# A late permutation in four wide matmuls, useless matmuls in TensorE's waits, and a residual moved behind the second MLP layer

## The chip, the cores and the metric

The kernel runs on one core of one Trainium2 chip. The metric is the device time of one execution in microseconds (us), given as the median of several executions.

Names in the profile: PE is TensorE's matmuls, PEld its weight loads, DVE is VectorE, ACT is ScalarE, SP the engine that issues transfers. The tiles: ring holds keys, values and weights as they land, PS is PSUM, O_sb is the copy of a unit's value result out of PSUM, SEL stands for the matmuls that pick that copy's rows by head, oTn the normalised result, KTb a work buffer, W2 the weights of the second MLP layer. A "fill" is a useless matmul.

## The reference, cut to what matters

One decoding step of a transformer block for 8 sequences: modulation, layer norm, attention of one new token over a cache of 8192 keys and values (8 key-value heads, 32 query heads, 128 wide), output projection and residual, then a second layer norm, a squared-ReLU MLP (512 to 1792 to 512) and the last residual.

```python
o = softmax(q @ k_cache.T / sqrt(128)) @ v_cache       # per batch and head; 268 MB of keys and values
x = x + ga * (o.reshape(B, 1, Hq * Dh) @ wo)
h = layernorm(x) * (1 + cb) + sb
x = x + gb * (relu(h @ w1 + b1) ** 2 @ w2 + b2)
```

## The kernel before

Keys and values stream through a ring of four 4 MB slots. For each batch there are four key units (transpose on TensorE, copy out, score), the softmax, and four value units. In the last batch the last value unit comes in chunks and is followed by the tail: projection of the last two heads, second layer norm, MLP, output. The parts that the change and the argument touch, with cuts marked:

```python
def pe_stream(n, at):      # n useless bf16 matmuls of 512 columns into bank `at`
def pe_stream32(n, at):    # the same in fp32: one each 0.94 us ahead of unit 2 in the trace before, against 0.22
...
# softmax of each batch
pe_stream32(1, 4)                                   # fills a wait for VectorE
T_ps = bank(7)[:, 0:4]
...
# value units p = 0..3 of a batch
def values(a, z, stop):                             # one matmul: 4 key tiles, 32 weight columns, 512 moving
    for m in range(a, z):
        cg = m % 4                                  # four column groups run beside each other
        t = op("tensor", lambda e, ...: e.matmul(Obank[32 * cg:32 * (cg + 1), :], lhs[...], vt[...],
               tile_position=(0, 32 * cg)), ...)
...
if p == NP - 3: pe_stream32(1, 4)                   # after unit 1's values
elif p == NP - 2: pe_stream(2, 4)                   # after unit 2's values
...                                                 # copy O_sb, four SEL matmuls
if p == NP - 3: pe_stream32(2, 4)                   # after unit 1's SEL, ahead of unit 2
...
# last value unit: CH = (64, 112, 120, 128)
t = values(16, 28, 24)                              # 12 matmuls
t = op("vector", ... tensor_copy(osb, bank(3)))     # copy O_sb
direct(CH[1], CH[2], 2)                             # one matmul per key tile, beside the copy
...                                                 # SEL, direct(CH[2], CH[3], 3), oTn
k_oP = permute(3, 4, oP[:, 0:2], [t])               # 16 matmuls of 16 columns, one copy of 128x64
...                                                 # 32 late projection matmuls, norm, first layer
for f in range(FT):                                 # second layer, 14 blocks of 4 matmuls
    if f == 8:
        ...                                         # residual: 4 matmuls of x1T with the identity
    for k in range(KT):
        t = op("tensor", ... matmul(yT_ps[:, k, :], W2v[:, f, ...], hidT[:, f, :]), [..., d_w2[f // 4]])
k_y2 = op("vector", ...)                            # y2, then 4 matmuls add it to the residual
```

## Time and profile before

| what | before |
|---|---|
| time, median of 3 (range) | 668.69 us (668.61 to 668.72) |
| span of the traced run | 666.6 us |
| first key transpose of the last batch | 585.91 us |
| clock back at full after it | 590.08 us |
| value unit 2 lands; its first matmul | 644.13; 644.18 us |
| last piece of W2 lands | 662.98 us |

The transfers fill the span; only the end of the last batch is compute that nothing hides. Two things help in reading the rest. First, everything behind value unit 2 is a single chain, so I give its events as distances from unit 2's first matmul. Second, TensorE's clock is full (1.00) or half (0.50), one value per window of 3.413 us. These are the windows in which the last batch's keys begin, before the change (after the stretch: busy time of PE, PEld, DVE, ACT and POOL with instruction counts, then granted clock, DMA share, GB/s):

```profile
583.25:586.67 3.42, 0.76 (x8) 0.77 (x9) 0.00 (x0) 0.00 (x0) 0.00 (x0) 0.50 1.07 460
586.67:590.08 3.41, 3.41 (x35) 3.41 (x34) 1.92 (x3) 1.02 (x1) 0.00 (x0) 0.50 0.96 413
590.08:593.49 3.41, 3.41 (x60) 2.88 (x59) 2.13 (x4) 2.33 (x3) 0.00 (x0) 1.00 0.98 423
```

And these are the early projection and the first value matmuls of the last unit behind it, at full clock, which c3 will be compared with:

```profile
649.11 1.48 PE PS L550 x24
650.59 0.86 PE PS L641 x16
```

In the windows above, the core waited for keys, fell to half clock, and got the full clock back 4.17 us after its first transpose: 35 matmuls in a window at half clock, 60 in the next.

### The profile page before, as it was taken

The page shows a single profiled execution, that of the slowest core. Times are in us where ns is not written, and L with a number is a line of the kernel's source. Part 1 is how long each engine was busy: PE and PEld are TensorE (multiplying, and loading weights), DVE is VectorE, ACT ScalarE, POOL GpSimd, SP SyncE. Part 2 cuts the span into 40 slices and gives each one's busy share as a digit, 9 for nine tenths or more (in the row PEclk, how much of TensorE's full clock was granted, in tenths as well). Part 3 has the DMA queues.
Part 4 walks back from the last instruction along what each step waited for, and adds up shares of the span by engine and source line. Part 5 has one row for each costly group of instructions (what it writes and reads, how often), then busy time and mean ns, then how long its engine had stood idle before and what let it go on. Part 6 is the DMA issues. An engine that isn't in the chain of part 4 may idle for free.

```text
span 666.6 us, 15803 instructions
## 1 busy us (share of the span) xinstructions
PE 518.3 (78%) x7201; PEld 350.3 (53%) x7201; DVE 308.0 (46%) x586; ACT 264.0 (40%) x305; POOL 20.4 (3%) x79
## 2 busy tenths in 40 slices
PE   3309987899769976699748987399776997589876
PEld 2207753677338742477317753287434773177534
DVE  1105662367326751367314663166523673156622
ACT  2104661265316651266314661156512663146620
POOL 7400000000000000000000000000000000000000
PEclk9999999799979999799987999799987999879996
DMA  9999999999999999999999999999999999999997
GB/s 377 435 412 437 419 429 432 429 433 435 433 427 433 438 427 433 431 433 431 431 436 427 433 433 436 429 429 435 433 431 431 436 429 431 433 436 427 431 425 283
DMA packets 12188, 283.85 MB, mean 426 GB/s; under 512 B 1260, under 2 KB 1296, under 8 KB 3600
## 3 DMA queue, kind: packets, MB, share of 16 engines
q1 hardware_dynamic: 12128, 283.65, 99.3%
q8 instruction: 9, 0.15, 0.1%
q10 hardware_dynamic: 48, 0.02, 0.0%
q14 instruction: 3, 0.02, 0.0%
HBM read 283.66 MB, written 0.01 MB: 426 GB/s over the span
## 4 chain that ended last, share of the span: by engine, by line
PE 55%; DMA 32%; ACT 6%; DVE 4%; issue 1%; POOL 0%; ACTq 0%; SPq 0%; DVEq 0%; POOLq 0%
PE PS L488 38%; DMA ring<-in_A_k_cache_dram 21%; PE PS L505 10%; DMA wo_sb<-in_A_wo_dram 7%; ACT P_sb L587 5%; DMA ring<-in_A_v_cache_dram 4%; PE PS L641 3%; ACT KTb L493 1%; DVE O_sb L659 1%; DVE m L512 1%; PE PS L599 1%; PE PS L550 1%; PE PS L619 0%; DVE Pm L613 0%; PE PS L478 0%
## 5 line engine op out<-in xcount | busy, mean ns | idle before, releaser
L488 PE MATMUL PS<-IDENT,ring 128*128 128x128 bf16 x4096 | 267.8, 228 | 60.7 <-DMA ring<-in_A_k_cache_dram 33.3
L488 PEld LDWEIGHTS PS<-IDENT,ring 128*128 128x128 bf16 x4096 | 247.3, 102 | 108.9 <-issue 49.4
L493 ACT ACTIVATE KTb<-PS 128x1024 bf16<-128x1024 bf16 x192 | 196.7, 1024 | 236.1 <-PE PS L488 236.1
L495 DVE COPY KTb<-PS 128x1024 bf16<-128x1024 bf16 x320 | 210.2, 688 | 151.6 <-PE PS L488 149.4
L505 PE MATMUL PS<-KTb,Qb 128*32 128x512 bf16 x1024 | 78.8, 384 | 4.5 <-ACT KTb L493 4.5
L641 PE MATMUL PS<-ring,Pm 128*32 128x512 bf16 x1020 | 66.9, 407 | 17.9 <-DMA ring<-in_A_v_cache_dram 15.2
L659 DVE CAST O_sb<-PS 128x512 bf16<-128x512 f32 x31 | 21.4, 692 | 106.9 <-PE PS L641 106.9
L641 PEld LDWEIGHTS PS<-ring,Pm 128*32 128x32 bf16 x1020 | 27.2, 102 | 53.5 <-DMA ring<-in_A_v_cache_dram 23.0
L542 ACT ACTIVATE KTb<-PS 32x192 bf16<-32x192 f32 x16 | 5.2, 322 | 103.6 <-PE PS L472 103.4
L587 ACT ACTIVATE P_sb<-PS,negm 128x1024 bf16<-128x1024 f32 x32 | 35.2, 1112 | 20.2 <-DVE negm L583 20.2
L478 PE MATMUL PS<-ONES 128*128 128x512 f32 x80 | 42.1, 630 | 0.0
L599 PE MATMUL PS<-IDENT,P_sb 128*128 128x128 bf16 x256 | 19.8, 220 | 17.2 <-ACT P_sb L587 17.2
L613 DVE COPY Pm<-PS 64x512 bf16<-64x512 bf16 x48 | 20.2, 421 | 25.0 <-PE PS L599 24.5
L599 PEld LDWEIGHTS PS<-IDENT,P_sb 128*128 128x128 bf16 x256 | 14.4, 98 | 27.9 <-ACT P_sb L587 27.9
L505 PEld LDWEIGHTS PS<-KTb,Qb 128*32 128x32 bf16 x1024 | 15.4, 94 | 21.0 <-ACT KTb L493 8.5
L512 DVE TENSOR_REDUCE m<-PS 128x1 f32<-128x512 f32 x32 | 22.1, 689 | 6.6 <-PE PS L505 6.6
L663 PEld LDWEIGHTS PS<-SEL,O_sb 128*128 128x128 bf16 x124 | 5.8, 97 | 31.3 <-DVE O_sb L659 31.3
L550 PE MATMUL PS<-wo_sb,KTb 128*32 128x512 bf16 x192 | 15.4, 467 | 6.8 <-ACT KTb L542 6.8
L663 PE MATMUL PS<-SEL,O_sb 128*128 128x8 bf16 x124 | 7.8, 169 | 14.1 <-DVE O_sb L659 14.1
L478 PEld LDWEIGHTS PS<-ONES 128*128 128x128 f32 x80 | 12.7, 190 | 10.6 <-issue 10.6
L472 PE MATMUL PS<-IDENT 128*128 128x512 bf16 x48 | 15.7, 381 | 0.0
L550 PEld LDWEIGHTS PS<-wo_sb,KTb 128*32 128x32 bf16 x192 | 5.9, 108 | 14.0 <-DVE KTb L544 9.5
(137 smaller groups left out, 147.1 us busy)
## 6 DMA issues: line engine op xcount, KB each, us to landing
ring<-in_A_k_cache_dram SPq DMA_DIRECT2D x32, 4096.0 KB, 31.4
ring<-in_A_v_cache_dram SPq DMA_DIRECT2D x31, 4096.0 KB, 27.4
ring<-in_A_wq_dram SPq DMA_DIRECT2D x1, 4096.0 KB, 20.1
wo_sb<-in_A_wo_dram SPq DMA_DIRECT2D x1, 4096.0 KB, 46.8
ring<-in_w_mod_dram SPq DMA_DIRECT2D x1, 3072.0 KB, 10.7
ring<-in_A_v_cache_dram SPq DMA_DIRECT2D x1, 2048.0 KB, 22.9
ring<-in_A_v_cache_dram SPq DMA_DIRECT2D x1, 1536.0 KB, 26.3
ring<-in_B_w_dram SPq DMA_DIRECT2D x3, 512.0 KB, 19.1
```

The lines of the kernel that those rows point to most:

```text
L478: ts = [op("tensor", lambda e: e.matmul(bank(at).rearrange("p (a r) -> p a r", a=4), ONES[:, :], rhs)) for _ in range(n)]
L488: t = op("tensor", lambda e, j=j, i=i: e.matmul(STG[j][:, i, :], src[:, 32 * k + 8 * j + i, :], IDENT[:, :], is_transpose=True), [loaded[n ...
L493: stg_free[j] = op("scalar", lambda e, j=j, dst=dst: e.activation(dst, STG[j], ACT.Copy), [t])
L495: stg_free[j] = op("vector", lambda e, j=j, dst=dst: e.tensor_copy(dst, STG[j]), [t])
L505: t = op("tensor", lambda e, hf=hf, q=q, rhs=rhs: e.matmul(PS[32 * q:32 * (q + 1), k, :], Qb[:, 2 * p + hf, :], rhs, start=(p == 0 and hf ...
L512: return op("vector", lambda e: e.tensor_reduce(m4[:, k:k + 1], bank(k), AX.X, ALU.max), [t])
L550: t = op("tensor", lambda e, g=g, j=j: e.matmul(bank(7)[32 * j:32 * (j + 1), :], oPe[:, 3 * (g % 2) + g // 2, :, :].rearrange("p j b -> p ...
L587: exps.append(op("scalar", lambda e, k=k: e.activation(P_sb[:, k, :, :, :], bank(k).rearrange("p (i x) -> p i x", i=8).unsqueeze(2).to_bro ...
L599: t = op("tensor", lambda e, k=k, i=i: e.matmul(STG[k][:, i, :], P_sb[:, k, i, :, :].rearrange("p h x -> p (h x)"), IDENT[:, :], is_transp ...
L613: done.append(op("vector", lambda e, dst=dst, frm=frm: e.tensor_copy(dst, frm), [t, k_pm]))
L641: t = op("tensor", lambda e, m=m, cg=cg, p=p, vt=vt, Obank=Obank: e.matmul(Obank[32 * cg:32 * (cg + 1), :], lhs[:, p, 32 * m:32 * m + 32], ...
L659: t = op("vector", lambda e, osb=osb, Obank=Obank: e.tensor_copy(osb, Obank), [t])
```

## The change

Its intent: fewer and wider matmuls in the last permutation, with its copy split over two engines; TensorE kept busy in the softmax and around value unit 2 so that its clock stays up; a chunk boundary moved; and the residual matmuls taken out of the middle of the second layer. The diff, cut to its core:

```diff
-        CH = (64, 112, 120, 128)
+        CH = (64, 104, 120, 128)
...
-        def permute(q0, q1, dst, deps):           # 16 matmuls into 4 column groups, one copy
-        def permute_early(deps):                  # 4 matmuls of 192 columns, one fill, 4 copies
+        def permute(pP, q0, q1, dst, deps, fill): # for both: 4 matmuls of 64*n columns, `fill` fills,
+                                                  # 2 copies on VectorE and 2 on ScalarE, 32 partitions each
...
             pe_stream32(1, 4)
+            pe_stream(1, 4)                       # twice in the softmax
...
-            turn_acts(pe_stream(2, 1))
+            turn_acts(pe_stream(3, 1))
...
-            pe_stream(1, 1)
+            pe_stream(2, 1)
...
-                    proj_done = project(permute_early([norm_last, k_all] + stg_free + hold))
+                    proj_done = project(permute(..., 0, 3, oPe, [norm_last, k_all] + stg_free + hold, 3))
...
                     elif p == NP - 2:
-                        pe_stream(2, 4)
+                        pe_stream(3, 4)
...
+                    elif p == NP - 2:             # after unit 2's SEL
+                        pe_stream(1, 4)
...
-                    t = values(16, 28, 24)
+                    t = values(16, CH[1] // 4, 22)
...
-                    k_oP = permute(3, 4, oP[:, 0:2], [t])
+                    k_oP = permute(bank(6)[:, 0:256]..., 3, 4, oP, [t], 0)
...
         for f in range(FT):
-            if f == 8:
-                ...                               # the four residual matmuls
             for k in range(KT):
                 ...
+        for cc in range(2):
+            ...                                   # the four residual matmuls
```

## The prediction

> **What bounds the kernel now.** I read the page's busy row and its DMA part first, then the chain that ended last in order of time, then the clock by windows.
>
> ```profile
> PE 518.3 (78%) x7201; PEld 350.3 (53%) x7201; DVE 308.0 (46%) x586; ACT 264.0 (40%) x305; POOL 20.4 (3%) x79
> ...
> q1 hardware_dynamic: 12128, 283.65, 99.3%
> ...
> HBM read 283.66 MB, written 0.01 MB: 426 GB/s over the span
> ```
>
> The DMA queue fills 99.3% of the span; no compute engine comes near. So the bulk of the 666.6 us is the time to read 283.66 MB, and the change reads the same bytes. Compute can matter only where it finishes after the data, so I followed the chain from the place where it last hangs on a transfer:
>
> ```profile
> 616.37 27.77 DMA ring<-in_A_v_cache_dram
> 644.13 0.04 issue
> 644.18 1.94 PE PS L641 x32
> ...
> 652.88 0.79 PE PS L641 x12
> ...
> 653.70 0.70 DVE O_sb L716
> ...
> 654.45 0.25 PE PS L719 x4
> 654.70 0.23 PE PS L693 x8
> ...
> 654.95 0.20 DVE oTn L723
> ...
> 655.20 0.39 PE PS L523 x14
> ...
> 655.61 0.24 DVE KTb L527
> ...
> 662.61 0.31 PE PS L774 x4
> 662.92 0.75 PE PS L778 x24
> ```
>
> Columns are start, length, what. The last value unit but one lands at 644.13; from there the chain is TensorE and VectorE work to the end, 22 us in which no step waits long for data. That is the only stretch where this change can move the time, so all it can win or lose is tenths of a microsecond of 668.69. The transfers are close behind the chain, though. The trace's semaphore records put the last chunk of values at 654.09 and the last piece of W2 at 662.98, and its last eight matmuls start near 663.3. In windows (after the stretch: each engine's busy time, then granted clock, DMA share, GB/s):
>
> ```profile
> 651.52:654.93 3.41, 2.89 (x51) 2.10 (x50) 0.69 (x1) 0.00 (x0) 0.00 (x0) 1.00 1.01 392
> 654.93:658.34 3.41, 1.75 (x56) 1.49 (x57) 1.35 (x8) 0.00 (x0) 0.00 (x0) 0.50 1.03 405
> ...
> 662.00:663.00 1.00, 1.00 (x32) 0.77 (x30) 0.14 (x1) 0.00 (x0) 0.00 (x0) 0.50 0.26 90
> 663.00:664.00 1.00, 0.72 (x26) 0.63 (x26) 0.19 (x1) 0.00 (x0) 0.00 (x0) 0.50 0.00 0
> ```
>
> The clock falls to 0.50 at 654.93 and stays there for the whole tail, and the DMA is in use until 663.
>
> **What the Trainium skill says.** (1) "TensorE: Matmul & The Clock Gate", Part 1: the clock is halved or full according to activity in a free-running window of 3413 ns. The trace agrees: all its changes lie at whole multiples of 3.413 us from each other (576.43, 579.84, 583.25, 590.08, 654.93). I added up, per window, the streamed columns at 2.4 GHz, weighted by the columns of the array in use: every window before a fall has at most 0.36 and every window that keeps the full clock 0.38 or more. The window 651.52 to 654.93 has 0.27; the two before it have 0.64. (2) Same page, same part: starts of small matmuls are never closer than about 25 ns. The trace agrees: eight-column matmuls follow each other every 25.0 ns at full clock and 26.7 ns at half, so half clock costs such matmuls only 7%; the 16-column ones take 33 ns instead. (3) "ScalarE: Activation LUTs", What ACT_TABLE_LOAD costs: 0.833 ns per element plus a fixed part. Here 192 elements took 322 ns (L542) and 256 took 375 (L793), 0.83 per element. The one table load in the tail took 1283 ns, as the page has it. (4) "PSUM — Partial Sum Buffer", Terms: two engines must not be in one bank and quadrant at once, different quadrants are allowed. The early copies (L542, L544) already run beside each other on such quadrants at 648.3, so the four late ones may too.
>
> **The change part by part.**
>
> *Useless matmuls.* A 128x512 bf16 matmul streams for 0.213 us (512 at 2.4 GHz). Softmax of each batch gets four more, unit 2 two more, the early permutation two more. Each sits in an idle piece of TensorE: after unit 2's values the copy O_sb takes 0.69 us (646.14 to 646.83), and three streams (0.64 us, begun at 646.02) end streaming by 646.66; behind the early permutation three end by 648.52, while its copies run to 648.97; in the softmax the gaps are 0.20, 0.72, 0.42 and 0.33 us against 0.21. Path: 0 (at worst 0.05). What they could buy is clock, but the windows they fill (up to 648.9) have 0.64 already, far over the 0.37 that decides, and the window that brings the fall begins at 651.52 and gets none. Gain: 0.
>
> *Chunks 64/104/120/128.* Two fewer of the 512-column value matmuls (12 to 10). Four run at once, 0.053 us each on average: 0.11 us less before the copy O_sb. Eight more direct matmuls (27 ns each) lie beside that copy's 0.69 us. The second chunk is 262 KB smaller and lands about 0.6 us earlier than 652.76, so no new wait. The weight of activity in the decisive window hardly changes (2 x 512 x 1/4 columns against 8 x 32: the same 256), so the clock still falls near 655. Path: -0.11.
>
> *Late permutation.* Before: 16 matmuls, 0.39 us, and one copy of 224 ns. After: 4 matmuls of 64 columns at half clock, 53 ns of streaming each and a record of about 0.21 us for the last: about 0.40 + 0.05. Then two copies in a row on each of two engines. VectorE: 64 elements took 224 ns (L527), twice with a 31 ns gap as at L544, 0.48 us. ScalarE: 375 less 192 x 0.83 gives 216 ns, twice plus some 0.04 of wait and gap, about the same. So copies 0.48 against 0.22, and permute +0.07. Path: +0.33. It is a loss. ScalarE's table load for the square root now comes behind these copies (about 656.2 to 657.5); it is needed at 660.19, so hidden.
>
> *Residual behind the second layer.* In the before-trace the last matmul of block 7 starts at 662.444 and the first of block 8 at 662.856: 0.41 us for four residual matmuls where a 26.7 ns step would do. Removing them wins 0.385 us in that place. The four now run in the 0.28 us between the last layer-2 matmul and y2, streaming about 0.21 us (two at a time, 107 ns at half clock): hidden. But with blocks 8 to 13 moved up, the last piece of W2 (landing 662.98, start possible at about 663.03) would be needed at 662.90: the transfer takes over. From 663.03 eight matmuls end at 663.41 instead of 663.66: at most -0.25 without help from upstream or from a faster DMA.
>
> *Sum.* Upstream: -0.11 + 0.33 = +0.22. Block 12 starts at 662.90 + 0.22 = 663.12, just behind its data; the end moves by 663.12 - 663.28 = -0.16 us. If the late permutation costs less, the W2 transfer holds the gain at -0.25, less some 0.04 that one larger piece instead of a 2 KB-per-row one may save (the two 262 KB chunks landed 0.65 to 0.68 us apart, 385 to 403 GB/s, against 410 to 423 for the pieces behind them). Centre: -0.2 us, so 668.5.
>
> **Rivals.** (a) *The clock stays up in the tail.* For it: the fall comes from a window that is only 0.10 short, and its phase is free-running, so in another run the fall could come up to 3.4 us later. Against: fills end before that window. If it happened, some 58 sixteen-column and other matmuls at 25 instead of 27 to 33 ns, and fixed parts, would save perhaps 0.5 us of TensorE time upstream, but W2's landing at 662.98 would cap the total at about -0.3: 668.4. The four runs before lie within 0.11 us, so phase cannot be worth much. (b) *The new copies on ScalarE wait longer* (a late wake-up, or the table load placed before them: 1.28 us). It would put the time at 668.8, or 669.5 with the load; the compiler places the load ahead of the instruction that needs it, so I give that 4%. (c) *Fills delay work*: unit 2's start at 644.18 follows fills that end at 644.08, so 0.1 us of delay in the softmax would show, but no more than 0.1: 668.6. (d) *Everything hidden by the transfer*: the last W2 landing decides and the time is 668.4.
>
> **Range and chances.** The four cases lie between 668.4 and 668.8; add 0.1 us of scatter as before and some for another chip: 668.2 to 668.85. Two per cent would be 13 us; nothing on the path is so large, so within 2% is 0.99.
>
> **What would show it.** In the changed trace, measured from unit 2's landing: the copy O_sb of the last unit 0.1 us sooner; from oTn to the first matmul of the late projection about 1.0 us instead of 0.75; the granted clock still 0.50 from a window's edge near 655; no gap between blocks 7 and 8 of layer 2, but a wait for the W2 transfer (or almost one) before block 12; y2 some 0.2 us sooner after W2's landing. I am wrong if the full clock lasts into the tail, if the late permutation is not slower, or if unit 2 itself starts late.

## More of the kernel before

The change and its causes are tenths of a microsecond in 668, so besides medians I use times within a trace, counted from one event of it.

L641 is line 641 of the kernel; lines shift by up to ten between versions, so I name the work as well.

## The result, and the profile after

| | before | changed |
|---|---|---|
| median of 4 runs | 668.71 us | 668.53 us |
| range | 668.61 to 668.81 | 668.20 to 669.24 |
| unit 2's first matmul (traced run) | 644.18 us | 645.25 us |
| from there to the end of the span | 22.47 us | 22.26 us |
| granted clock falls in the tail | 654.93 us | 656.84 us |

The ratio is 0.9999, with a 95% interval of 0.9981 to 1.0016. Ratios here are the mean time of one kernel's runs over that of the other's of the same rounds, so they are not quite the ratio of the medians.

Two things stand beside each other. The tail became 0.21 us shorter. But the traced run of the changed kernel is its slowest, 669.24 us, and there unit 2 began 1.07 us later than in the trace before: its data landed 0.65 us later (644.79 against 644.13), and it started 0.41 us after landing plus 0.05. The chain of the changed kernel in order of time (start, length, what) shows both:

```profile
643.42 0.08 PE PS L658 x4
643.50 1.82 PE PS L478 x4
645.32 1.87 PE PS L634 x32
...
653.96 0.77 PE PS L634 x10
...
654.75 0.70 DVE O_sb L713
...
656.01 0.20 DVE oTn L720
...
656.25 0.30 PE PS L522 x4
...
656.58 0.21 DVE KTb L535
...
656.83 0.23 DVE KTb L535
657.06 0.12 issue
657.18 1.01 PE PS L727 x32
...
662.86 1.66 PE PS L769 x56
664.52 0.31 PE PS L774 x4
664.83 0.41 PE PS L782 x4
```

Read it against the chain shown in the prediction. Before, a transfer stood ahead of unit 2; here it is L478, the useless fp32 matmuls, that unit 2 follows. (A piece of the chain begins where the record before it ends, here 645.32; the first matmul itself started at 645.25.) Ten value matmuls (L634) take 0.77 us where twelve took 0.79. The late permutation (L522) takes 0.30 us, then two copies of 0.21 and 0.23 in a row, so the late projection starts 1.17 us after oTn did, against 0.94 before. The second layer (L769) is one piece of 1.66 us, and the residual (L774) comes behind it.

The windows of the changed kernel at the start of the last keys, and in its tail:

```profile
585.16:588.57 3.41, 2.03 (x20) 2.03 (x21) 0.69 (x1) 0.10 (x1) 0.00 (x0) 0.50 1.03 442
588.57:591.98 3.41, 3.41 (x35) 3.41 (x34) 1.48 (x3) 1.88 (x2) 0.00 (x0) 0.50 0.94 404
591.98:595.39 3.41, 3.41 (x59) 2.74 (x61) 2.38 (x4) 2.04 (x3) 0.00 (x0) 1.00 1.01 432
...
653.42:656.84 3.42, 2.55 (x47) 1.67 (x46) 1.11 (x4) 0.23 (x2) 0.00 (x0) 1.00 1.03 401
656.84:660.25 3.41, 2.04 (x60) 1.91 (x61) 1.29 (x7) 1.48 (x2) 0.00 (x0) 0.50 1.03 411
```

The full clock came back at 591.98, 5.44 us after the first transpose (586.54), instead of 4.17. Half clock costs half of that time: 2.72 against 2.08 us. The keys themselves landed 0.63 us later than in the other trace. Together that is 1.27 us; unit 0's values started 1.24 us later (637.56 against 636.32).

### The profile page after: what moved, and what is told of

Its sections match the earlier page's. It is cut to its first block, busy times and chain, and to the rows that moved or that the text cites. A ratio compares the mean times of both kernels' runs of the same rounds, so it can differ in the third digit from the quotient of the medians.

```text
span 667.5 us, 15923 instructions
## 1 busy us (share of the span) xinstructions
PE 524.1 (79%) x7259; PEld 351.0 (53%) x7259; DVE 308.1 (46%) x587; ACT 264.6 (40%) x307; POOL 20.5 (3%) x79
## 4 chain that ended last, share of the span: by engine, by line
PE 59%; DMA 29%; ACT 7%; DVE 3%; issue 1%; POOL 0%; ACTq 0%; SPq 0%; DVEq 0%; POOLq 0%
PE PS L488 39%; DMA ring<-in_A_k_cache_dram 22%; PE PS L505 10%; DMA wo_sb<-in_A_wo_dram 7%; ACT P_sb L580 5%; PE PS L634 4%; PE PS L478 2%; ACT KTb L493 1%; DVE O_sb L654 1%; PE PS L472 1%; PE PS L592 1%; DVE Pm L606 1%; PE PS L612 0%; PE PS L541 0%; PE PS L658 0%
## 5 line engine op out<-in xcount | busy, mean ns | idle before, releaser
L634 PE MATMUL PS<-ring,Pm 128*32 128x512 bf16 x1018 | 64.6, 396 | 20.8 <-DMA ring<-in_A_v_cache_dram 20.0
L634 PEld LDWEIGHTS PS<-ring,Pm 128*32 128x32 bf16 x1018 | 26.1, 99 | 55.8 <-DMA ring<-in_A_v_cache_dram 28.4
L533 ACT ACTIVATE KTb<-PS 32x192 bf16<-32x192 f32 (+1 forms) x18 | 5.6, 311 | 109.9 <-PE PS L472 103.1
L478 PE MATMUL PS<-ONES 128*128 128x512 f32 x80 | 42.1, 630 | 0.0
L472 PE MATMUL PS<-IDENT 128*128 128x512 bf16 x112 | 33.4, 380 | 0.0
L478 PEld LDWEIGHTS PS<-ONES 128*128 128x128 f32 x80 | 12.7, 190 | 10.6 <-issue 10.6
L472 PEld LDWEIGHTS PS<-IDENT 128*128 128x128 bf16 x112 | 9.9, 103 | 10.1 <-issue 7.2
L541 PE MATMUL PS<-wo_sb,KTb 128*32 128x512 bf16 x192 | 11.8, 380 | 3.4 <-ACT KTb L533 3.4
```

The costliest lines, as they stand in the source:

```text
L472: ts = [op("tensor", lambda e: e.matmul(bank(at).rearrange("p (a r) -> p a r", a=4), IDENT[:, :], rhs)) for _ in range(n)]
L478: ts = [op("tensor", lambda e: e.matmul(bank(at).rearrange("p (a r) -> p a r", a=4), ONES[:, :], rhs)) for _ in range(n)]
L634: t = op("tensor", lambda e, m=m, cg=cg, p=p, vt=vt, Obank=Obank: e.matmul(Obank[32 * cg:32 * (cg + 1), :], lhs[:, p, 32 * m:32 * m + 32], ...
```

## The experiments

My theory: the median moves by the sum of the parts (residual, late permutation, chunks), the added fills lie beside other work, and the runs' spread comes from the phase of the clock's windows. Rivals: the fills hold the clock and are the whole gain, or the transfers make the spread. Twelve kernels ran, all correct, in three groups; each group ran on one chip with its own runs of the kernel before (medians 668.98, 669.00 and 668.79 us). The executions scatter by more than a part of the change is worth, so each part's verdict rests on its trace, counted from unit 2's start, and the executions are given beside it.

### a1: the changed kernel once more

No edit.

> The changed kernel once more, for the scatter and a second trace. Theory (clock phase): what differs between its runs is when TensorE gets its full clock back in the first scores of the last batch; in the trace of 669.24 us that was at 591.98 us, against 590.08 us in the trace of the kernel before, and value unit 2 then started 1.07 us later. Expected: runs from 668.2 to 669.3 us, and in the new trace a start of unit 2 at 644.2 to 645.3 us that goes with the time of the clock's return. Rival (transfers): the runs differ because one of the DMA engines lags (unit 2's last landing was 0.66 us later in the slow trace); then the start of unit 2 follows the landing within 0.1 us whatever the clock did.

Measured: 669.23, 668.70, 668.54, 668.32 and 669.20 us. In the trace (669.23) the clock came back at 592.28, unit 2 landed at 644.50 and started at 645.25. So the start did not follow the landing; it was 0.70 us later than landing plus 0.05. The transfers alone do not explain it.

The traces fit one formula. Unit 2 starts at the later of (landing + 0.05) and (first transpose + half of the time to the clock's return + 55.99). The constant is set on the first changed trace; the second gives 586.26 + 3.01 + 55.99 = 645.26, measured 645.25. In the trace before, 585.91 + 2.08 + 55.99 = 643.98 lies before the landing: no delay. Two more traces test it, each with two fp32 fills: a3 gives 644.44, measured 644.45, and c3, a padded version of the kernel before, gives 645.30, measured 645.29, 0.57 us late. So the clock decides whether the two fp32 fills ahead of unit 2 are free, and the late start is not a property of the change: the kernel before has it at the same phase.

### a2: the residual alone

```diff
 # from the kernel before
-            if f == 8: (four residual matmuls)
+        (the four residual matmuls behind the loop over f)
```

> The kernel before with the residual matmuls moved behind layer 2 and nothing else. Theory: 0.25 to 0.40 us less than before (668.3 to 668.45 us), blocks 0 to 13 of layer 2 in one run of 1.66 us. If the last piece of W2 takes over, a wait before block 12 and only 0.25 us. Rival (residual hidden anyway or y2 delayed by it): no gain.

Measured: median 668.79 us beside 668.98, ratio 0.9995 (0.9982 to 1.0009). The executions alone would not settle 0.2 us; the trace does. The end is 22.21 us after unit 2's start, against 22.47. The second layer:

```profile
661.76 1.77 PE PS L772 x56
663.53 0.31 PE PS L777 x4
```

It takes 1.77 us and not 1.66, because block 12 starts 0.127 us after block 11 where a step is 0.027: the last piece of W2 landed at 663.12. Both halves of the prediction's step hold, the gain and the transfer that takes over.

### a3: the late permutation alone

```diff
 # from the kernel before
-k_oP = permute(3, 4, oP[:, 0:2], [t])                 # 16 matmuls, one copy
+k_oP = permute(bank(6)[:, 0:256]..., 3, 4, oP, [t], 0) # 4 matmuls, 4 copies
```

> The kernel before with the late permutation in four matmuls and four copies and nothing else. Theory: 0.2 to 0.35 us more than before (668.9 to 669.05 us); from oTn to the first late projection matmul 0.95 to 1.1 us instead of 0.75. Rival (the four matmuls save as much as the copies add): the time of before.

Measured: median 668.90 us beside 668.98, ratio 0.9998 (0.9984 to 1.0012); the median shows nothing. In the trace the late projection starts 1.18 us after oTn did (0.94 before), and the end is 22.70 us after unit 2's start, 0.23 more:

```profile
655.22 0.20 DVE oTn L716
...
656.40 1.01 PE PS L723 x32
```

The sum of a2 and a3 in the traces is -0.26 + 0.23 = -0.03 us; the changed kernel has -0.21, and its second layer has no gap for W2 (1.66 us), because the permutation's cost already puts it behind the transfer. So the two parts do not simply add: the layer is 0.40 us shorter there, and in a2 0.29. The rest is small: the second layer starts 17.61 us after unit 2 in the changed kernel, 17.65 in a3 and 17.42 before, and 0.19 - 0.40 is the -0.21. It is not the clock: the late projection ran at half clock in all three of these traces, a matmul every 26.7 ns on average.

### a4: the changed kernel without the added fills

```diff
 # from the changed kernel: bf16 fills as in the kernel before
-after unit 2's values 3, after its SEL 1, early permutation 3, in the softmax 1, 1, 3 and 2
+after unit 2's values 2, after its SEL 0, early permutation 1, in the softmax 0, 0, 2 and 1
```

> The changed kernel without the added useless matmuls. Theory: they do nothing, the median is that of the changed kernel within 0.15 us (668.4 to 668.7 us), and the clock falls at a window's edge between 654 and 658 us as with them. Rival (the fills hold the clock): 0.3 us or more slower than the changed kernel, with a fall of the clock before 652 us in the trace.

Measured: median 668.41 us (668.33 to 668.54), ratio 0.9989 (0.9975 to 1.0003). The end is 22.20 us after unit 2's start. The fills bring nothing to the usual run.

### b1, b2: one and three fp32 fills ahead of unit 2

```diff
 # from the changed kernel, after unit 1's SEL
-pe_stream32(2, 4)
+pe_stream32(1, 4)     # b1;  3 in b2
```

> The changed kernel with one fp32 fill (0.98 us on TensorE) ahead of value unit 2 instead of two. Theory (clock phase times fills): unit 2 starts at the later of its landing + 0.05 us and first key transpose + half of the time until the clock's return + 56.0 us; the late runs (669.2 us) are late because the fills still run when unit 2 lands. One fill less takes 0.98 us from the second term, which then is never the later one: all five runs between 668.1 and 668.7 us, unit 2 starting within 0.1 us of its landing in the trace. Rival (the fills hold the clock, or the scatter comes from the transfers): still runs above 669 us.

> The changed kernel with three fp32 fills ahead of value unit 2 instead of two. Theory: 0.98 us more in the second term; with the clock's return 2.6 to 6.0 us after the first transpose, unit 2 starts 0 to 1.7 us after its landing, so the median is 0.4 to 1.0 us above that of the changed kernel (669.0 to 669.6 us) with runs up to 670.2 us. Rival (fills hidden in the wait for unit 2): the time of the changed kernel.

Measured, b1: 668.22 to 668.71 us, median 668.49; no run above 669, as expected. Its timeline shows TensorE waiting for the landing again:

```profile
644.16 1.91 PE L634 MATMUL PS<-ring,Pm 128*32 128x512 bf16 x32 [1.30 <-DMA ring<-in_A_v_cache_dram]
```

Measured, b2: 668.24, 668.56, 668.68, 669.70 and 670.01 us. The median lies below the 669.0 that I expected, but the range goes up as expected. Its chain:

```profile
641.90 2.68 PE PS L478 x6
644.58 1.87 PE PS L634 x32
```

The clock had come back early here (3.03 us after the first transpose), and still unit 2 followed the fills, 0.17 us after its landing (the first matmul started at 644.51). The formula with 0.98 us more gives 644.59. Three of the traced kernels with one fill, b4, c1 and c4, had the clock back after 5.92, 5.17 and 3.42 us, and none had a delay of unit 2. This settles the start after the landing: fills times clock phase, not transfers. A late landing comes on top.

### b3: the kernel before with one fp32 fill

```diff
 # from the kernel before, after unit 1's SEL
-pe_stream32(2, 4)
+pe_stream32(1, 4)
```

> The kernel before with one fp32 fill ahead of unit 2 instead of two and nothing else. Theory: it loses its late runs (669.1 to 670.8 us among nine) and keeps the others: all runs from 668.5 to 669.0 us. Rival: scatter as before.

Measured: 668.77, 668.85, 669.59, 670.24 and 670.65 us. A miss. The trace (668.85) is in order, so the reason for the slow ones is not in it. But 670 us is also seen in the kernel before itself: 4 of its 33 runs lay between 670.24 and 671.03 us. Unit 2's lateness is at most about 0.7 us; these runs must have another cause. c3 shows one that could be it; no slow run of b3 or of the kernel before was traced.

### b4: the residual, old permutation, chunks in full rows, one fill

```diff
 # from the kernel before
-CH = (64, 112, 120, 128) ... t = values(16, 28, 24) ... pe_stream32(2, 4)
+CH = (64, 96, 120, 128)  ... t = values(16, 24, 20) ... pe_stream32(1, 4)
 # and the residual as in a2
```

> A version of its own: the old late permutation (16 matmuls, one copy), the residual behind layer 2, chunks 64/96/120/128 so that the last value matmuls come in two full rows of four instead of three, one fp32 fill less. Theory: the copy O_sb of the last unit 0.21 us sooner than before, measured from unit 2's start (9.3 us), the first late projection matmul at about 11.5 us; but the last W2 piece (landing 18.8 us after unit 2's start) then holds blocks 12 and 13, so the end stays at 22.2 us, as with the residual alone, and the runs lie from 668.1 to 668.5 us. Rival (the transfers do not bind): another 0.2 us less, 22.0 us.

Measured: 669.11 to 670.19 us, median 669.82. Worse than everything else, though the path is what I wanted: O_sb's copy starts 9.31 us after unit 2 (9.52 before), the late projection at 11.48. Then:

```profile
649.12 15.11 DMA ring<-in_B_w_dram
664.23 0.04 issue
664.28 0.38 PE PS L772 x8
```

The last two blocks waited for W2 until 664.23. Fifteen of the sixteen parts of that transfer had landed by 662.99. The packets of the trace show one of 16384 bytes of the instruction queue, in flight from 661.95 to 663.04, and then the last four packets of W2, which end at 663.81. In the trace before, the same fetch began at 662.24, and W2's last packets had ended by 662.57, not behind it. The trace does not name a packet's DMA engine; that the four stood behind the fetch is read from the times. The two fetches of 16384 bytes in the tail took 1.06 to 1.11 us in all fourteen traces.

### c1, c2, c3: is it the place of the fetch in the program?

```diff
 # c1: b4 without its chunks      c2: b4, and ahead of the loop      c3: the kernel before, and ahead of the loop
+for _ in range(116):   # c2; 12 in c3
+    op("tensor", lambda e: e.matmul(bank(4)[:, 0:8], IDENT[:, :], IDENT[:, 0:8]), [k_modT])
```

> The version of b4 without its chunks (so before, with the residual behind layer 2 and one fp32 fill less). In b4's trace a 16 KB instruction fetch (661.95 to 663.04 us) stood before the last four W2 packets of one DMA engine, and W2 landed 1.24 us later than on the other fifteen. Theory A (the fetch): without the chunks' 12 more matmuls (24 instructions[...]) in the last part the fetch comes later in the program, behind W2 as in the other traces: 668.2 to 668.7 us in all five runs. Theory B (one fp32 fill less does it; it is also in the slow runs of b3): runs of 669 us and more again.

> b4 with 116 small useless matmuls ahead of the loop, where TensorE waits for the first keys anyway[...]. Theory A (the place of the fetch in the program): b4 becomes fast, 668.1 to 668.6 us, end 22.2 us after unit 2's start. Theory B (its earlier path or its chunks make it slow, whatever the blocks): still 669.1 to 670.2 us.

> The kernel before with 12 small useless matmuls ahead of the loop (24 instructions), the shift that the chunks of b4 bring. Theory A: slow runs as b4's become common, median 0.5 to 1.3 us above before. Theory B: the time of before within 0.2 us.

Measured: c1 has four of six runs from 668.42 to 668.59, the others at 669.06 and 669.68 (median 668.59). c2 stays slow, 669.43 to 670.19. c3 is slow, 669.50 to 669.56 and once 671.30. By the times, c1 speaks for theory A in four runs of six and for B in two, c3 for A, c2 for B. The traces say something else. Those of c2 and c3 have one fetch more than the others (at 28.1 us, after the padding), so the padding did more than shift, and W2 lands last on two engines: at 664.13 and 664.99 in c2, at 663.65 and 664.07 in c3. In c2 the last four W2 packets again follow a fetch (662.69 to 663.78) and end at 664.56, so the padding did not take the fetch out of the way, and c2 says nothing against the fetch as a cause. In c3 no W2 packet follows one; one engine just ends late (packets in an unbroken row to 663.66). So it is in the changed kernel's own trace, where fifteen parts of W2 landed by 662.81 and the last at 663.63, and was not waited for. That a fetch held W2 back is seen in b4's and c2's traces; why b4, c2 and c3 are slow in every run stays open.

The run of 671.30 us is the one that was traced, and it shows something else:

```profile
646.82:650.23 3.41, 1.90 (x23) 0.68 (x16) 1.58 (x4) 0.79 (x3) 0.00 (x0) 1.00 0.99 420
650.23:653.65 3.42, 3.42 (x36) 1.44 (x40) 0.63 (x1) 1.14 (x1) 0.00 (x0) 0.50 0.99 388
```

and in its chain the early projection:

```profile
650.22 2.75 PE PS L553 x24
652.97 1.26 PE PS L644 x16
```

The clock fell at 650.23, just where the projection begins: 2.75 us instead of 1.48, and 1.26 instead of 0.86 in the trace before. Those two are 1.67 us. The window that brought the fall is the one around value unit 2, with a streamed share of 0.36, counted as in the prediction. I then slid such a window over the traces. In the kernel before, windows that end 4.9 to 5.2 us after unit 2's start have 0.35 to 0.37; in the changed kernel no window that ends from 2 to 9.4 us after it has less than 0.51. So by this count the added fills close a gap that only some phases meet: some 0.3 to 0.5 us of the 3.413, which is an estimate of one run in seven to eleven. The count is rough: over all fourteen traces windows between 0.35 and 0.38 went either way, and in c1's trace one that ends 4.9 us after unit 2's start had 0.36 and kept the clock. The 4 of 33 slow runs of the kernel before would fit, but none of them was traced. None of the 14 runs of the changed kernel and of b1 was above 669.24. But a2, a4 and c4 have the same gap and had no slow run in 15, so how much the fills win in the mean is not shown by the times. What is shown is the early fall and its cost, in one trace; that the fills prevent it is worked out and not measured.

### c4: no added fills, one fp32 fill

```diff
 # a4, and after unit 1's SEL
-pe_stream32(2, 4)
+pe_stream32(1, 4)
```

> The changed kernel without any of the added fills and with one fp32 fill less ahead of unit 2. By the sum of the parts (residual and late permutation stay, fills do nothing, no late unit 2): 668.2 to 668.6 us in all five runs, the best of all versions or equal to b1 and a4. Rival: a clock that falls earlier for want of fills, 0.3 us slower.

Measured: 668.06 to 668.67 us, median 668.30 beside 668.79 for the kernel before, ratio 0.9984 (0.9969 to 1.0000). The slowest is the traced one, with the keys 0.4 us late; its tail is 22.23 us. It has the lowest median of all, and its interval touches 1. By the sliding window it is not safe from the early fall; b1 is (668.49).

## Why the prediction was right or wrong

**The size was right.** Predicted 668.5 us, measured 668.53; predicted a tail 0.2 us shorter, measured 0.21. That the medians agree to 0.03 us is luck: the four runs lie 1.04 us apart, and one, 669.24, is outside the stated range. The tail is the better test. The steps did not all hold:

- *Useless matmuls, path 0*: right. From the last batch's first softmax fill to unit 0's first value matmul it took 8.90 us before and after, and the early projection starts 4.93 us after unit 2 in both.
- *Useless matmuls, gain 0*: right for the usual run (a4), wrong as a rule. "The windows they fill (up to 648.9) have 0.64 already" was read from the one phase of one trace. A sliding window finds 0.35 there, and c3's traced run lost 1.67 us to it.
- *Chunks, -0.11*: wrong; the copy O_sb started 0.02 us sooner. "Four run at once, 0.053 us each on average" failed: twelve matmuls are three rows of four, and so are ten. Eight are two rows: b4 won 0.21 us. The chunk did land earlier, 8.0 us after unit 2's start in a4 instead of 8.6.
- *Late permutation, +0.33*: a loss, as said, but +0.23 (a3). The copies were right (0.48 expected, 0.47 measured). The matmuls were over-sized: 0.30 us at full clock, not 0.45 at half, as the fall came just behind them. Left out was a longer idle time between the last copy and the first late projection matmul, 0.13 us against 0.06.
- *Residual, -0.385, at most -0.25 where W2 binds*: right. The layer went from 2.06 to 1.66 us in the changed kernel, and a2 hit the transfer and stopped at -0.26.
- *The sum*: -0.02 + 0.23 - 0.40 is -0.19. Two errors of about 0.1 us, the chunks too good and the permutation too bad, cancelled.
- *"Phase cannot be worth much"*: wrong. It rested on runs that lie within 0.11 us, and these were three, not four; the fourth, 668.81, came with the result. In the traces phase was worth 0.7 us through the start of unit 2 (a1), and 1.67 through an early fall (c3). Rival (c) named the right place with the wrong culprit: the old fp32 fills, not the new ones.

## What to carry to other kernels

A filler that is free at one clock phase stands in the way at another: size it against the latest possible start of what follows, and check the activity of every window phase, not only of the one in the trace. Work that runs in rows of four is counted in rows. And before shortening a tail, see which transfer, instruction fetches included, lands just behind it.

## What the Trainium skill lacked or had wrong

- "TensorE: Matmul & The Clock Gate", Part 1, gives no share of activity at which the clock falls; it speaks of idle windows. Here a window in which the profile shows PE busy for 2.89 of 3.41 us brought the fall. By streamed columns, windows of 0.36 and less fell in the trace before and those of 0.38 kept the clock; over all fourteen traces windows from 0.35 to 0.38 did either. It also advises not to fit to a particular count of cold matmuls, as the ramp is under 1% of a span. Here the window's phase was worth 0.7 us by a late return (a1) and 1.67 us in c3's trace: under 1% too, but more than the whole change.
- The same page, Part 4, says that the full clock does not engage for transposes, as they do not count as busy in the same way. Here the window 586.67 to 590.08 held only transposes (35 matmuls, half clock), and the next had the full clock.
- "Runtime: NRT & Kernel Launch", Instruction fetch mechanics, tells that the sequencer fetches blocks of 16 KiB, 256 instructions, through a DMA queue of its own, and calls the cost of crossing such a boundary mostly hidden. It gives no time for a fetch and does not say that one can delay data. Here a fetch of 16384 bytes took about 1.1 us, and in b4 the last four packets of W2 came behind one, landing 1.24 us after the other fifteen parts.
